# Attention and channel mix on one core: q transposes that write words in sequence, a permuted token order and a new order of the work

## The chip, the cores and the metric

The kernel runs on one core of a Trainium2 chip. The core has five engines that run side by side, each with its own queue of instructions: TensorE (PE, matmuls; PEld is its weight load), VectorE (DVE), ScalarE (ACT), GpSimd (POOL) and SyncE (SP). Data move between DRAM and the on-chip memories by DMA; SP, ACT and POOL issue the DMAs, and 16 DMA engines carry them. The metric is the device time in microseconds, lower is better.

## The reference

For each of 8 batches, 8 heads, 576 tokens and a head size of 64, linear attention without a softmax and a norm over each head's 64 values:

```python
kv = np.einsum('bhsd,bhse->bhde', k, v)
out = np.einsum('bhsd,bhde->bhse', q, kv)
rms = np.sqrt(np.mean(out * out, axis=-1, keepdims=True) + 1e-06)
x = out / rms * g_norm                      # then heads side by side: (8, 576, 512)
```

Then a channel mix, in which each token is blended with the token before it (zero for the first):

```python
x_prev = np.concatenate([np.zeros((B, 1, D)), x[:, :-1, :]], axis=1)
xk = mu_k * x + (1.0 - mu_k) * x_prev
xr = mu_r * x + (1.0 - mu_r) * x_prev
k = np.maximum(xk @ w_k, 0.0)               # 512 -> 1024
v = k * k @ w_v                             # 1024 -> 512
r = 1.0 / (1.0 + np.exp(-(xr @ w_r)))
return r * v
```

Inputs and outputs are float32; inside, the matmuls take bfloat16.

## The kernel before

**Attention, batch by batch.** The names of the pieces carry the batch, then the head group z (z = 0 is heads 0 to 3, z = 1 heads 4 to 7; batch 0 does the two apart, the later batches do both in one piece, "01"), then a half.

- `ld.` loads k, v, q and the weights with a cast to bfloat16 by POOL's DMA queue (L226, L221, L252). For batch 0, z = 0, k and v come as float32 by SP (`ldh`, L236) and are cast by DVE and ACT (`cst`, L128, L130). `small` loads the two mu vectors (each as 4 rows) and the g vector twice (one row each) by SP (L193 to L197); `tr9` turns them on PE (L211) and `cols` copies them (L200).
- `kv` multiplies k and v on PE (L265); `kc` copies the result out of PSUM, `ks` splits it by even and odd d on PE (L271) and `kd` copies it again (the copies at L128 or L130).
- `tq` transposes q on DVE in blocks of 32 x 32 words of 32 bits, a word being two bfloat16 values (L350). A q tile holds 128 partitions: 8 heads of 16 partitions (QP), each with 36 consecutive tokens (QJ) of 64 values. After the transpose a block's 32 columns are 2 heads x 16 partitions for one of the 36 token numbers j. There are two pieces a batch and z group, each with 18 of the 36 j.
- `u` multiplies the transposed q by kv on PE (L281), for one half of the columns at a time. `uc` scales it by g into uT (L134, L136), `sq` squares it (L371), `ss` sums the squares on PE (L396, L380), `rs` takes the reciprocal root on ACT (L286); from batch 2 on, one `rs` serves all heads and `sp` spreads it by 4 DMAs per z on SP (L418).
- `mul` makes x (L393), `d` is x minus the x before it (L298), `mk` and `mr` scale it by mu (L134, L136), `xk` and `xr` add x (L311). They go into rings of 4 batches of columns.

**Channel mix, group by group.** A group is 512 columns of the rings, whatever batch they belong to (9 groups). `k` (L494; group 0 in quarters at L470), `relu` (L453), `ksq` (L481, L504), `r` (L516), `sig` (L526), `v` (L536), `out` = v times sig (L549, L563), `st` stores 128 rows (L444). PSUM has four tiles of two banks in a ring ("ps"); a piece that needs a tile waits until the tile four back has been read.

**The order.** `ORDER` (L15) is a string with the name of each piece in the order in which it is emitted, some with the engine to be used after an @ (A is ACT, D is DVE). Each engine runs its own instructions in this order and waits where data or a buffer are not there. `z:512` is a matmul on zeros that adds nothing and keeps PE busy (L438); there are 38, and `zz` is another (the trace has 39 weight loads and 37 matmul records of them).

In the kernel before, the transpose writes each block's words with a step of 36 words, so that a head's 576 columns stand in the order of the tokens:

```python
dst = get(qT).rearrange("q t r -> q (t r)").bitcast(FP32).rearrange("q (p j) -> q j p", j=QJ)
```

A half of u then needs both transposes of its z, the token before is the column before, and a store writes 128 rows of DRAM that follow each other.

Of the kernel before, what the change touches and what calls it, by code (L numbers as in the profile page):

```python
# [15 lines left out]
ldh.v ldh.k table seta setp perm ld.q0.0 ld.q0.1 ident ld.k0.1 ld.v0.1 ld.wk1 ld.wk0 ld.k1.0 ld.q1.01 ld.v1.0 ld.v1.1 ld.k1.1 ld.wv0 ld.wv1 ld.wr ld.q2.01 ld.v2.01 ld.k2.01 zz cst.v0@D cst.k1@A small setb cst.v1@D tq0.0.1 tq0.0.0 cst.k0@A z:512 z:512 z:512 z:512 z:512 z:512 z:512 z:512 z:512 z:512 z:512 z:512 z:512 z:512 z:512 z:512 z:512 kv0.0 tr9 cols kc0.0@A ks0.0 kd0.0@A z:512 z:512 z:512 z:512 z:512 u0.0.0 sq0.00 u0.0.1 tq0.1.1 uc0.01@A uc0.00@D z:512 z:512 ss0.00 rs0.00 tq0.1.0 z:512 z:512 kv0.1 ld.k3.01 ld.v3.01 ld.q3.01 kc0.1@A sq0.01 z:512 z:512 ks0.1 kd0.1@A z:512 z:512 u0.1.1 u0.1.0 sq0.10 uc0.10@A z:512 z:512 z:512 ss0.10 rs0.10 mul0.00 d0.00 mk0.00@D xk0.00 mr0.00@D z:512 ss0.01 rs0.01 z:512 z:512 z:512 z:512 k0.000 mul0.10 d0.10 sq0.11 ss0.11 mk0.10@D uc0.11@A mul0.01 xk0.10 k0.001 rs0.11 d0.01 mul0.11 d0.11 mk0.01@A mk0.11@A xk0.11 k0.010 xk0.01 tq1.01.1 relu0.00 k0.011 xr0.00 k0.110 k0.111 mr0.11@A xr0.11 relu0.01 ksq0.01 ksq0.00 relu0.11 tq1.01.0 ld.q4.01 k0.100 k0.101 mr0.10@A kv1.01 ld.v4.01 ld.k4.01 relu0.10 ksq0.11 ksq0.10 kc1.01@A ks1.01 kd1.01@A u1.01.1 uc1.11@A uc1.01@D sq1.11 mr0.01@D v0.3.0 xr0.01 u1.01.0 uc1.10@D v0.2.0 sq1.00 uc1.00@D v0.3.1 sq1.01 xr0.10 ss1.0 sq1.10 ss1.3 ss1.1 rs1.0 rs1.1 mul1.0 v0.2.1 d1.0 rs1.3 ss1.2 rs1.2 r0.0 r0.1 sig0.0 r0.2 mul1.1 d1.1 mk1.1@D mr1.1@D xk1.1 tq2.01.1 r0.3 v0.0.0 v0.0.1 mk1.0@A v0.1.0 xk1.0 v0.1.1 mr1.0@A sig0.1 out0.0 k1.4 kv2.01 ld.k5.01 kc2.01@A ks2.01 kd2.01@A tq2.01.0 ld.q5.01 ld.v5.01 u2.01.1 sq2.11 out0.1 uc2.01@D sq2.01 uc2.11@D k1.5 k1.0 u2.01.0 relu1.2 sq2.00 uc2.10@D sq2.10 uc2.00@D k1.1 k1.6 kv3.01 ld.k7.01 ss2 rs2 sp2.0 k1.7 kc3.01@D ks3.01 relu1.0 ksq1.2 sp2.1 xr1.1 xr1.0 kd3.01@A k1.2 k1.3 tq3.01.1 relu1.3 r1.2 relu1.1 tq3.01.0 ksq1.3 ksq1.1 r1.3 sig1.1 u3.01.1 sq3.11 r1.0 st0.0 r1.1 ksq1.0 sig1.0 uc3.01@A v1.3.0 uc3.11@D tq4.01.1 v1.2.0 v1.2.1 sq3.01 u3.01.0 sq3.10 uc3.00@A sq3.00 v1.0.0 v1.1.0 v1.3.1 kv4.01 ld.k6.01 ld.q7.01 ld.v6.01 mul2.0 uc3.10@A ss3 d2.0 mk2.0@D rs3 v1.1.1 v1.0.1 kc4.01@A xk2.0 ks4.01 kd4.01@A mul2.1 d2.1 mk2.1@D xk2.1 k2.4 k2.0 out1.1 mr2.1@D tq4.01.0 ld.q6.01 ld.v7.01 mr2.0@A xr2.0 st0.2 st0.1 out1.0 k2.2 k2.3 relu2.1 xr2.1 k2.1 ksq2.1 sp3.1 st1.3 relu2.0 ksq2.0 k2.5 relu2.2 tq5.01.1 k2.6 k2.7 relu2.3 u4.01.0 uc4.00@D sp3.0 v2.2.0 uc4.10@A r2.2 sq4.00 r2.3 ksq2.2 sig2.1 sq4.10 ksq2.3 r2.0 r2.1 sig2.0 st0.3 v2.3.0 mul3.1 d3.1 tq5.01.0 mul3.0 kv5.01 kc5.01@A d3.0 u4.01.1 sq4.01 uc4.01@D v2.2.1 v2.3.1 sq4.11 st1.0 mk3.0@D mr3.1@A uc4.11@A out2.1 xk3.0 v2.0.0 st1.2 ks5.01 mk3.1@D xk3.1 kd5.01@A v2.1.0 u5.01.0 sq5.00 uc5.10@A mr3.0@D ss4 sq5.10 uc5.00@A v2.1.1 xr3.0 rs4 v2.0.1 k3.0 k3.2 k3.3 relu3.1 tq7.01.1 sp4.0 k3.1 sp4.1 xr3.1 out2.0 st2.1 ksq3.1 relu3.0 r3.2 ksq3.0 r3.3 u5.01.1 r3.0 sig3.1 tq6.01.0 r3.1 uc5.11@D sq5.11 uc5.01@D k3.4 k3.5 st1.1 st2.0 tq6.01.1 mul4.0 d4.0 sig3.0 relu3.2 ksq3.2 sq5.01 k3.6 k3.7 kv6.01 relu3.3 ksq3.3 kc6.01@A kv7.01 kc7.01@D ss5 mr4.0@A rs5 v3.2.0 mk4.0@D st2.2 v3.2.1 ks7.01 kd7.01@A mul4.1 ks6.01 v3.3.0 kd6.01@A v3.3.1 v3.0.0 d4.1 mk4.1@D mr4.1@D xk4.1 u6.01.1 sq6.11 v3.0.1 uc6.01@A sp5.0 v3.1.0 v3.1.1 sq6.01 uc6.11@A u6.01.0 sq6.00 sp5.1 uc6.10@A out3.1 st3.3 xr4.0 xk4.0 k4.2 out3.0 k4.3 sq6.10 relu4.1 st2.3 tq7.01.0 uc6.00@D k4.4 ksq4.1 k4.5 relu4.2 ksq4.2 k4.6 u7.01.1 ss6 xr4.1 rs6 mul5.0 d5.0 uc7.01@D k4.7 relu4.3 mr5.0@D k4.0 k4.1 relu4.0 sp6.0 r4.0 ksq4.3 mul5.1 sq7.11 st3.2 sq7.01 r4.1 sig4.0 r4.2 r4.3 ksq4.0 v4.3.0 d5.1 mr5.1@D v4.3.1 mk5.1@D uc7.11@A mul6.0 v4.2.0 sig4.1 u7.01.0 sq7.10 mk5.0@D xk5.0 v4.2.1 sp6.1 out4.1 st4.2 st4.3 xk5.1 v4.1.0 v4.1.1 mul6.1 sq7.00 ss7 rs7 sp7.1 v4.0.0 d6.1 v4.0.1 uc7.00@A uc7.10@D mk6.1@D d6.0 k5.2 xr5.0 mk6.0@D xk6.0 xk6.1 k5.0 k5.1 xr5.1 mul7.1 sp7.0 k5.4 k5.5 relu5.0 relu5.2 k5.3 relu5.1 ksq5.0 k6.6 ksq5.1 k6.7 relu6.3 mr6.1@D k6.4 v5.2.0 k6.5 relu6.2 k6.0 k6.1 k5.6 d7.1 out4.0 ksq6.3 k5.7 mr7.1@A v5.0.0 mr6.0@D xr6.0 v5.3.0 ksq5.2 relu5.3 relu6.0 ksq6.0 mk7.1@A r5.0 r5.1 xk7.1 sig5.0 r5.2 r5.3 sig5.1 xr6.1 st3.0 ksq5.3 v5.1.0 v5.3.1 v5.0.1 mul7.0 d7.0 mk7.0@A xk7.0 r6.0 r6.1 sig6.0 k6.2 k6.3 relu6.1 ksq6.1 v5.1.1 out5.0 k8.2 r6.2 xr7.1 ksq6.2 k8.3 k7.2 v5.2.1 relu8.1 k7.0 k7.1 r6.3 relu7.0 st3.1 out5.1 ksq7.0 st4.0 st5.1 k7.3 mr7.0@A xr7.0 v6.2.0 v6.3.0 v6.3.1 sig6.1 v6.0.0 v6.2.1 v6.0.1 st4.1 out6.1 st6.3 k7.6 k7.7 relu7.1 ksq7.1 r8.0 relu7.3 ksq7.3 r8.1 sig8.0 k7.4 k8.6 k8.7 relu8.3 k7.5 relu7.2 k8.0 v6.1.0 st6.2 ksq7.2 v6.1.1 v7.1.0 out6.0 ksq8.3 v7.1.1 st6.1 st6.0 v7.0.0 r7.0 r7.1 v7.0.1 sig7.0 v7.2.0 v7.2.1 out7.0 st5.3 ksq8.1 st7.1 k8.4 k8.5 st5.0 r7.2 relu8.2 st7.0 k8.1 relu8.0 r7.3 ksq8.0 sig7.1 r8.2 r8.3 sig8.1 ksq8.2 v8.1.00 v7.3.0 v7.3.1 st5.2 v8.1.10 out8.10 st8.10 out7.1 st7.2 v8.0.00 v8.0.10 out8.00 v8.2.00 v8.2.10 out8.20 v8.3.00 st7.3 v8.3.10 st8.00 v8.3.01 v8.3.11 st8.20 out8.30 st8.30 out8.31 st8.31  # L16
# [40 lines left out]
def kernel(  # L57
# [32 lines left out]
    X0 = 2  # L90
# [12 lines left out]
        "qT": (2, (128, 2 * S, 2), BF16),  # L103
# [66 lines left out]
    def setup_b(_):  # L170
        nc.vector.memset(eps, 1e-6)
        nc.vector.memset(ones, 0.0)
        for e in range(2):
            nc.vector.memset(ones[64 * e:64 * e + 64, 64 * e:64 * e + 64], 1.0 / HD)
        nc.vector.memset(heads, 0.0)
        for e in range(2):
            nc.vector.memset(heads[64 * e:64 * e + 64, e::2], 1.0 / HD)
        for x in xTs:
            nc.vector.memset(x[:, :, 0:X0], 0.0)

# [93 lines left out]
    def u_tiles(pss, kv, qT, zs, c0, c1):  # L274
        for r in range(2):
            for z in zs:
                for y in range(2):
                    for e in range(2):
                        m = 2 * z + y
                        rows_ = slice(32 * m, 32 * m + 32)  # L280
                        nc.tensor.matmul(pss[z][64 * e:64 * e + 64, y, 0:c1 - c0], kv[rows_, r, HD * e:HD * e + HD],  # L281
                                         qT[rows_, S * e + c0:S * e + c1, r], start=(r == 0), stop=(r == 1))
# [5 lines left out]
    x_ready, x_free = {}, {}  # L288
# [3 lines left out]
    def blends(b, z, name, x0, w, deps, mds, dd):  # L292
        xT = xTs[(NZ * b + z) % NX]
        cur, prev = slice(X0 + x0, X0 + x0 + w), slice(X0 - 1 + x0, X0 - 1 + x0 + w)
        cs, r0 = slice(x0, x0 + w), S * (b % RB) + x0
# [23 lines left out]
    PARTS = ((0, GA), (GA, S))  # L319

    def parts(b):
        return PARTS if b == 0 else ((0, HS), (HS, S))

    def attention(b):
# [7 lines left out]
        for zs in zss:  # L332
# [12 lines left out]
            for i in range(2):  # L345
                def tq(_, i=i, part=part):
                    src = qin.t.bitcast(FP32).rearrange("q (j i) -> q j i", i=32)
                    dst = get(qT).rearrange("q t r -> q (t r)").bitcast(FP32).rearrange("q (p j) -> q j p", j=QJ)
# [8 lines left out]
        for i, (c0, c1) in enumerate(parts(b)):  # L357
            for zs in zss:
                p = add(f"u{b}." + "".join(map(str, zs)) + f".{i}", "T", lambda _, zs=zs, i=i, c0=c0, c1=c1: u_tiles(
                    {z: get(us[z][i]) for z in zs}, kv.t, qT.t, zs, c0, c1),  # L360
                    deps=sum(([*qd[z], kvcs[z]] for z in zs), []), bufs=[us[z][i] for z in zs] + [qT, kv])
                for z in zs:
                    pu[(z, i)] = p
        secs = {}
        for z in range(NZ):
            for i, (c0, c1) in enumerate(parts(b)):
# [21 lines left out]
        for z in range(NZ):  # L388
# [51 lines left out]
    out_rows = out.rearrange("b s c -> (b s) c")  # L440
# [164 lines left out]
```

## Time and profile before

| what | value |
|---|---|
| three runs | 202.07, 202.88 and 202.91 us, median 202.88 |
| the profiled execution | 202.8 us as timed; span from first to last instruction 201.0 us |
| granted TensorE clock | 1.000 |
| DVE busy, of it transposes (18 instructions) | 138.3 us, 21.3 us |
| fillers on zeros | 37 matmul records, 12.4 us |
| first matmul of the mix, last matmul ends | 18.57 us, 197.16 us |
| DMA | 30.63 MB in 21016 packets; HBM read 33.56 MB, written 9.44 MB |
| stores | 37 DMAs: 35 of 256 KB and 2 of 128 KB |

How to read the profile's lines: times are microseconds from the start of the span unless "ns" is said. A group's line has the kernel's line, the engine, the operation, the tile written, an arrow and the tiles read, the shapes and the number of instructions; then the busy time and the mean of one in ns; then the idle time of the engine just before them and what ended it. In the slices each digit is the busy share of a fortieth of the span in tenths. A line of the chain has start, duration and what ran. A line of the windows has the window, its length, the busy time of PE, PEld, DVE, ACT and POOL with the number of instructions, the granted clock, the share of the 16 DMA engines' time that was busy, and GB/s. The share can come out a little over 1, since packets on an engine overlap.

### The profile page before, as it was taken

Reading aid. Unit: us, or ns where it says so; the run is one execution under the profiler, and the core shown is the slowest. Engines: PE = TensorE matmul, PEld = TensorE weight load, DVE = VectorE, ACT = ScalarE, POOL = GpSimd, SP = SyncE. Lnnn points to the kernel's source line nnn. Section 1 sums busy time; section 2 is a strip of 40 time slices with the busy share of each in tenths; the row PEclk is TensorE's granted clock in tenths of the full one; section 3 lists DMA queues with packets and bytes.
Section 4 is the critical chain, followed back from the end, with each engine's and each line's share of the span. In section 5 each row is a group of like instructions: output and inputs, shape, how many; then the busy total and the mean of one; then the engine's idle time right before and its main releaser. Section 6 shows DMA issues by size and latency. Waiting matters only on the chain.

```text
span 201.0 us, 4245 instructions
## 1 busy us (share of the span) xinstructions
PE 189.8 (94%) x1743; PEld 93.9 (47%) x1765; DVE 138.3 (69%) x229; ACT 129.5 (64%) x172; POOL 23.1 (12%) x41
## 2 busy tenths in 40 slices
PE   7999779988999999999999999999999999999992
PEld 2545664443544444544545754444444444444451
DVE  1596687997879999797897798998454423133252
ACT  2367978957998579898968689375963554312500
POOL 7743331212100500000000000000000000000000
PEclk9999999999999999999999999999999999999999
DMA  6999999999999999999614242551000202045044
GB/s 212 198 210 216 201 206 216 203 207 219 207 230 257 246 250 265 238 213 194 230 26 94 105 124 50 165 163 57 0 0 0 104 3 104 0 157 209 0 151 166
DMA packets 21016, 30.63 MB, mean 152 GB/s; under 512 B 1917, under 2 KB 14469, under 8 KB 20997
## 3 DMA queue, kind: packets, MB, share of 16 engines
q0 software_dynamic: 11264, 16.19, 45.1%
q1 hardware_dynamic: 9588, 14.03, 21.9%
q8 instruction: 14, 0.23, 0.4%
q10 hardware_dynamic: 144, 0.13, 0.2%
q14 instruction: 6, 0.04, 0.1%
HBM read 33.56 MB, written 9.44 MB: 214 GB/s over the span
## 4 chain that ended last, share of the span: by engine, by line
PE 73%; DMA 9%; DVE 8%; ACT 4%; issue 2%; POOL 2%; SPq 1%; POOLq 0%; DVEq 0%
PE ps L536 27%; PE ps L494 26%; PE ps L516 12%; DMA w_k<-in_moe_w_k_dram 6%; DMA rs<-rsc 3%; PE ps L281 2%; DVE out L549 2%; DVE qT L350 2%; PE ps L470 1%; PE ps L265 1%; ACT relu L453 1%; ACT md L134 1%; DVE xk L311 1%; SPq L418 1%; PE ps L380 1%
## 5 line engine op out<-in xcount | busy, mean ns | idle before, releaser
L536 PE MATMUL ps<-w_v,sqk 128*128 128x512 bf16 (+1 forms) x286 | 65.8, 373 | 0.8 <-issue 0.3
L494 PE MATMUL ps<-xk,w_k 128*128 128x512 bf16 (+1 forms) x282 | 58.2, 355 | 0.7 <-issue 0.3
L453 ACT ACTIVATE relu<-ps 128x1024 bf16<-128x1024 f32 x36 | 36.2, 1022 | 27.9 <-PE ps L494 27.5
L536 PEld LDWEIGHTS <-sqk 128*128 128x128 bf16 x296 | 28.0, 98 | 32.8 <-issue 2.4
L494 PEld LDWEIGHTS <-w_k 128*128 128x128 bf16 x288 | 27.7, 98 | 27.5 <-issue 1.5
L504 DVE TENSOR_TENSOR sqk<-relu 128x1024 bf16<-128x1024 bf16 x32 | 21.6, 687 | 21.5 <-ACT relu L453 21.4
L516 PE MATMUL ps<-w_r,xr 128*128 128x512 bf16 x140 | 33.2, 379 | 0.2
L549 DVE TENSOR_TENSOR out<-ps,sig 128x1024 f32<-128x1024 f32 x16 | 19.5, 1220 | 11.5 <-PE ps L536 7.3
L371 ACT ACTIVATE sq<-ps 128x576 bf16<-128x576 f32 (+2 forms) x32 | 20.3, 650 | 9.1 <-PE ps L281 8.0
L526 ACT ACTIVATE sig<-ps 128x1024 bf16<-128x1024 f32 x18 | 18.3, 1022 | 8.5 <-PE ps L516 7.8
L350 DVE STREAM_TRANSPOSE qT<-q 128x576 f32<-128x576 f32 (+1 forms) x18 | 21.3, 1201 | 2.5 <-DMA q<-in_q_dram 2.1
L516 PEld LDWEIGHTS <-xr 128*128 128x128 bf16 x144 | 13.9, 98 | 16.6 <-issue 0.5
L134 ACT ACTIVATE md<-d,cols 128x576 bf16<-128x576 bf16 (+2 forms) x26 | 16.7, 698 | 0.5 <-DVE d L298 0.5
L144 ACT ACT_TABLE_LOAD x12 | 15.4, 1283 | 0.9 <-PEq L589 0.7
L136 DVE TENSOR_SCALAR uT<-ps,cols 128x576 bf16<-128x576 f32 (+1 forms) x16 | 12.5, 801 | 4.4 <-PE ps L281 2.2
L393 DVE TENSOR_TENSOR xT<-uT,rs 128x1152 bf16<-128x1152 bf16 (+2 forms) x18 | 12.3, 685 | 3.6 <-ACT rs L286 3.5
L311 DVE TENSOR_TENSOR xk<-md,xT 128x1152 bf16<-128x1152 bf16 (+2 forms) x18 | 12.2, 687 | 3.4 <-ACT md L134 3.2
L136 DVE TENSOR_SCALAR md<-d,cols 128x576 bf16<-128x576 bf16 (+2 forms) x46 | 13.9, 354 | 0.2
L438 PE MATMUL ps<-zero 128*128 128x512 bf16 x37 | 12.4, 477 | 1.5 <-DVE zero L164 1.2
L298 DVE TENSOR_TENSOR d<-xT 128x1152 bf16<-128x1152 bf16 (+2 forms) x18 | 12.5, 692 | 0.5
L311 DVE TENSOR_TENSOR xr<-md,xT 128x1152 bf16<-128x1152 bf16 (+2 forms) x18 | 12.1, 683 | 0.7 <-ACT md L134 0.6
L134 ACT ACTIVATE uT<-ps,cols 128x576 bf16<-128x576 f32 (+2 forms) x16 | 11.9, 743 | 0.6 <-PE ps L281 0.6
(47 smaller groups left out, 105.9 us busy)
## 6 DMA issues: line engine op xcount, KB each, us to landing
out_dram<-out SPq DMA_DIRECT2D x35, 256.0 KB, 2.4
q<-in_q_dram POOLq DMA_DIRECT2D x7, 576.0 KB, 21.4
v<-in_v_dram POOLq DMA_DIRECT2D x6, 576.0 KB, 21.9
k<-in_k_dram POOLq DMA_DIRECT2D x6, 576.0 KB, 20.5
rs<-rsc SPq DMA_DIRECT2D x48, 72.0 KB, 2.8
w_k<-in_moe_w_k_dram POOLq DMA_DIRECT2D x2, 512.0 KB, 11.3
w_v<-in_moe_w_v_dram POOLq DMA_DIRECT2D x2, 512.0 KB, 16.1
k<-in_k_dram POOLq DMA_DIRECT2D x3, 288.0 KB, 12.8
```

What stands on the lines that cost most here:

```text
L134: nc.scalar.mul(out=dst, in_=src, mul=col)
L136: nc.vector.tensor_scalar(out=dst, in0=src, scalar1=col, scalar2=None, op0=ALU.mult)
L311: nc.vector.tensor_tensor(out=dst[:, 2 * z:2 * z + 2, r0:r0 + w], in0=md.t[:, :, cs], in1=xT[:, :, cur], op=ALU.add)
L350: nc.vector.transpose(out=dst[part, js, :], in_=src[part, js, :])
L371: sq_ = add("sq" + name, "A", lambda _, ps=ps, sq=sq, cs=cs, w=w: nc.scalar.activation(out=get(sq)[:, :, cs], in_=ps.t[:, :, 0:w], func=AF ...
L453: nc.scalar.activation(out=get(rt), in_=ps.t, func=AF.Relu)
L494: nc.tensor.matmul(get(ps)[:, fc % 2, a0:a1], w_k_sb[:, cc, 128 * fc:128 * fc + 128], xk[:, cc, x0:x0 + a1 - a0], start=(cc == 0), stop=(c ...
L504: nc.vector.tensor_mul(out=get(sqk)[:, 2 * f2:2 * f2 + 2, :], in0=rt.t, in1=rt.t)
L516: nc.tensor.matmul(get(ps)[:, ci % 2, :], xr[:, cc, n0:n0 + 128], w_r_sb[:, cc, :], start=(cc == 0), stop=(cc == NHP - 1))
L526: nc.scalar.activation(out=get(sg), in_=ps.t, func=AF.Sigmoid)
L536: nc.tensor.matmul(get(ps)[:, bank, cs], sqk.t[:, fc, 128 * ci:128 * ci + 128], w_v_sb[:, fc, cs], start=(fc == 0), stop=(fc == NFC - 1))
L549: dv = add(f"out{g}.{c2}", "D", lambda _, ps=ps, sg=sg, ot=ot: nc.vector.tensor_mul(out=get(ot), in0=ps.t, in1=sg.t), deps=ms + [sg_done], ...
```

## The change

The transposes write their words in sequence: a block's 32 columns now stand side by side, and the columns of a head are ordered by j first and partition second. Column c of a batch holds token 36 * (c mod 16) + c // 16. What follows from it:

- The columns of one transpose piece are exactly one half of u, and u waits for this piece alone; u reads 18 runs of 16 columns of its head. Batch 0 is cut into halves of 288 too, where it was cut at 256.
- The token before stands 16 columns back. For the first 16 columns (j = 0) it is in the last 16, one partition lower; `mul` copies these into 15 columns ahead of the tile, by a second small `tensor_mul` for each batch and z.
- In batch 0, whose halves are blended apart, the first 16 columns wait for the second half: they become a third blend (`d0.02`, `mk0.02`, `mr0.02`, `xk0.02`, `xr0.02` and the same for z = 1), and stand last in the ring, so that they belong to group 1.
- A store's 128 rows are now up to 8 values of j with 16 tokens each, 36 rows of DRAM apart. A tile of rows that spans two batches, or the end of batch 0's order, is stored by two or three DMAs: one tile by three and three tiles by two, 42 DMAs in all with the halved last one.
- `ORDER` is another one: the loads come in another order, there are 37 fillers beside `zz` where there were 38, and pieces stand elsewhere all through it, some on the other engine.

The diff, with the ORDER cut to the opening, the first steps of the mix and the end, and broken into lines here:

```diff
 ORDER = """
-ldh.v ldh.k table seta setp perm ld.q0.0 ld.q0.1 ident ld.k0.1 ld.v0.1 ld.wk1 ld.wk0 ld.k1.0 ld.q1.01 ld.v1.0 ld.v1.1 ld.k1.1
-ld.wv0 ld.wv1 ld.wr ld.q2.01 ld.v2.01 ld.k2.01 zz cst.v0@D cst.k1@A small setb cst.v1@D tq0.0.1 tq0.0.0 cst.k0@A (17 z:512)
-kv0.0 tr9 cols kc0.0@A ks0.0 kd0.0@A (5 z:512) u0.0.0 sq0.00 u0.0.1 tq0.1.1 uc0.01@A uc0.00@D
...
-k0.000 mul0.10 d0.10 sq0.11 ss0.11 mk0.10@D uc0.11@A mul0.01 xk0.10 k0.001 rs0.11 d0.01 mul0.11 d0.11 mk0.01@A mk0.11@A xk0.11
-k0.010 xk0.01 tq1.01.1 relu0.00 k0.011 xr0.00 k0.110 k0.111 mr0.11@A xr0.11 relu0.01 ksq0.01 ksq0.00 relu0.11 tq1.01.0 ld.q4.01
-k0.100 k0.101 mr0.10@A kv1.01 ld.v4.01 ld.k4.01 relu0.10 ksq0.11 ksq0.10 kc1.01@A ks1.01 kd1.01@A u1.01.1 uc1.11@A uc1.01@D
-sq1.11 mr0.01@D v0.3.0 xr0.01 u1.01.0
...
-kv2.01 ld.k5.01 kc2.01@A ks2.01 kd2.01@A tq2.01.0 ld.q5.01 ld.v5.01 u2.01.1
...
-v8.1.00 v7.3.0 v7.3.1 st5.2 v8.1.10 out8.10 st8.10 out7.1 st7.2 v8.0.00 v8.0.10 out8.00 v8.2.00 v8.2.10 out8.20 v8.3.00 st7.3
-v8.3.10 st8.00 v8.3.01 v8.3.11 st8.20 out8.30 st8.30 out8.31 st8.31
+ldh.k ldh.v ld.q0.0 table seta setp ident perm ld.q0.1 ld.k0.1 ld.v0.1 ld.wk0 ld.v1.1 ld.wk1 ld.k1.0 ld.v1.0 ld.k1.1 ld.wr
+ld.q1.01 ld.wv0 ld.wv1 ld.k2.01 ld.v2.01 ld.q2.01 small zz (8 z:512) tr9 cst.v0@D cst.k0@A cst.v1@D cst.k1@A (6 z:512)
+kv0.0 setb tq0.0.1 kc0.0@A tq0.1.1 (2 z:512) ks0.0 kd0.0@A (2 z:512) u0.0.1 sq0.01 tq0.0.0 (4 z:512) u0.0.0 cols uc0.01@D sq0.00
...
+ss0.11 k0.000 rs0.11 k0.010 mul0.11 mk0.10@A k0.110 d0.11 xk0.10 mr0.11@A k0.100 mk0.11@D k0.001 xr0.01 xk0.11 xr0.10 k0.011
+relu0.00 xr0.11 k0.101 xr0.00 kv1.01 relu0.10 ksq0.10 kc1.01@A relu0.01 k0.111 ks1.01 mr0.02@D kd1.01@D ksq0.00 r0.2 relu0.11
+r0.3 sig0.1 mk0.02@D r0.0 r0.1 ksq0.11 sig0.0 tq1.01.1 u1.01.1 sq1.11 tq1.01.0 ld.q4.01 ld.v4.01 ld.k4.01 uc1.01@D u1.01.0
...
+kv2.01 ld.k5.01 ld.v5.01 kc2.01@A ks2.01 kd2.01@A tq2.01.0 tq2.01.1 ld.q5.01 mr1.1@A k1.4 k1.5 u2.01.0
...
+kv6.01 relu3.1 relu3.3 mul4.0 d4.0 ksq3.1 ss5
...
+v8.2.00 v8.0.00 v7.0.0 v7.0.1 out7.0 st7.1 st7.0 v8.1.00 v8.2.10 out8.20 st8.20 v8.1.10 v8.0.10 out8.10 st8.10 out8.00 st8.00
+v8.3.00 v8.3.10 out8.30 st8.30 v8.3.01 v8.3.11 out8.31 st8.31
 """
...
-    X0 = 2
+    X0 = QP
...
-        "qT": (2, (128, 2 * S, 2), BF16),
+        "qT": (2, (128, QJ, 2 * QP, 2), BF16),
...
-            nc.vector.memset(x[:, :, 0:X0], 0.0)
+            nc.vector.memset(x[:, :, 0:1], 0.0)
...
-    def u_tiles(pss, kv, qT, zs, c0, c1):
+    def u_tiles(pss, kv, qT, zs, js):
...
-                        nc.tensor.matmul(pss[z][64 * e:64 * e + 64, y, 0:c1 - c0], kv[rows_, r, HD * e:HD * e + HD],
-                                         qT[rows_, S * e + c0:S * e + c1, r], start=(r == 0), stop=(r == 1))
+                        nc.tensor.matmul(pss[z][64 * e:64 * e + 64, y, 0:HS], kv[rows_, r, HD * e:HD * e + HD],
+                                         qT[rows_, js, QP * e:QP * e + QP, r], start=(r == 0), stop=(r == 1))
...
-        cur, prev = slice(X0 + x0, X0 + x0 + w), slice(X0 - 1 + x0, X0 - 1 + x0 + w)
-        cs, r0 = slice(x0, x0 + w), S * (b % RB) + x0
+        cur, prev = slice(X0 + x0, X0 + x0 + w), slice(x0, x0 + w)
+        cs, r0 = slice(x0, x0 + w), S * (b % RB) + ((x0 - QP) % S if b == 0 else x0)
...
-                    dst = get(qT).rearrange("q t r -> q (t r)").bitcast(FP32).rearrange("q (p j) -> q j p", j=QJ)
+                    dst = get(qT).rearrange("q j p r -> q (j p r)").bitcast(FP32).rearrange("q (j p) -> q j p", j=QJ)
...
-                    deps=sum(([*qd[z], kvcs[z]] for z in zs), []), bufs=[us[z][i] for z in zs] + [qT, kv])
+                    deps=sum(([qd[z][i], kvcs[z]] for z in zs), []), bufs=[us[z][i] for z in zs] + [qT, kv])
...
                 nc.vector.tensor_mul(out=xT[:, :, X0 + cs.start:X0 + cs.stop], in0=uT.t[:, :, cs], in1=rs.t[:, :, cs])
+                if cs.stop == S:
+                    nc.vector.tensor_mul(out=xT[:, :, 1:QP], in0=uT.t[:, :, S - QP:S - 1], in1=rs.t[:, :, S - QP:S - 1])
...
+                done = blends(b, z, f"{b}.{z}2", 0, QP, muls, mds[z], dd)
...
-    out_rows = out.rearrange("b s c -> (b s) c")
+    out_jt = out.rearrange("b (t j) c -> b j t c", j=QJ)
...
     def store(g, ci, ot, cs=slice(None), eng=None):
-        row = G * g + 128 * ci
-        (eng or nc.sync).dma_start(out=out_rows[row:row + 128, cs], in_=ot)
+        p = 0
+        while p < 128:
+            b, c = divmod(G * g + 128 * ci + p, S)
+            j = (c // QP + 1) % QJ if b == 0 else c // QP
+            n = min(8 - p // QP, QJ - j, (S - c) // QP)
+            (eng or nc.sync).dma_start(out=out_jt[b, j:j + n, :, cs], in_=ot[p:p + QP * n])
+            p += QP * n
...
```

Words such as "(17 z:512)" stand for so many fillers in a row.

## Prediction

> **What bounds the kernel now.** I read the page's busy table and slices first, then the chain that ended last in order of time, the groups by form, the DMA queues, and windows of the tail. Durations come from the profiled execution: span 201.0 us, 202.8 us as timed, 0.08 below the median of the three runs (202.88), so span + 1.8 is the time.
>
> ```profile
> PE 189.8 (94%) x1743; PEld 93.9 (47%) x1765; DVE 138.3 (69%) x229; ACT 129.5 (64%) x172; POOL 23.1 (12%) x41
> ...
> PE   7999779988999999999999999999999999999992
> ...
> DMA  6999999999999999999614242551000202045044
> ```
>
> PE is full from slice 9 on (45 us); what can be won lies before that, what can be lost in the last slice and wherever a load comes late. The DMA engines are full until 93 us.
>
> ```profile
> 5.93 12.60 DMA w_k<-in_moe_w_k_dram
> 18.53 0.05 issue
> 18.57 1.05 PE ps L470 x8
> ...
> 42.68 1.22 DVE out L549
> ...
> 67.54 7.07 PE ps L494 x32
> ...
> 188.33 8.83 PE ps L536 x48
> 197.16 0.02 issue
> 197.19 0.42 DVE out L563
> ```
>
> The first useful matmul of the mix (piece k0.000) waits for w_k until 18.57; the chain then changes engines until 67.54, and is PE alone from there to 197.16. PE's work from k0.000 on, at 0.216 us for 512 columns (24 matmuls of L536 take 5.18 us of the chain): L536 62.2, L494 55.3, L516 31.1, L470 6.9, the kv, split, u and ss pieces 15.4, together 170.9 us. Without a wait it would end at 189.5; it ends at 197.16. Of the 7.7 us, 1.3 fall after 67.54, where PE never waits: that is what my per-matmul figures are short. **6.4 us are waits before 67.54**: 1.7 within k0 (xk of half 1 late at 23.81), 2.0 between kv1 and the first v piece (copies on ACT with nothing for PE between), 2.0 around kv2 and u2 (copies; PSUM held until DVE has freed it), 0.7 later.
>
> **The change, part by part.**
>
> ```profile
> L350 DVE STREAM_TRANSPOSE qT<-q 128x576 f32<-128x576 f32 x14 | 16.7, 1203 | 0.4 <-PE ps L281 0.4
> ...
> L350 DVE STREAM_TRANSPOSE qT<-q 64x576 f32<-64x576 f32 x4 | 4.6, 1193 | 2.2 <-DMA q<-in_q_dram 2.1
> ...
> L130 DVE CAST v<-xk 128x576 bf16<-128x576 f32 x2 | 0.9, 456 | 3.2 <-DMA xk<-in_v_dram 3.2
> ```
>
> *Transposes.* 1.2 us for 576 words a lane is 2.1 ns a word, written 144 bytes apart. No row shows a sequential write; the bounds are the plain copy of 576 words (0.46) and today's 1.20. I take 0.65, nearer to the copy, since a transpose differs from it only in the order of its words. That is 18 x 0.55 = 10 us of DVE time. The 16 added copies of 15 columns cost at least the 0.06 us of the smallest memset, batch 0's third blend some 14 such instructions more: 2 us. After 67.54 the 8 us are worth nothing: PE is late there, not DVE.
>
> *u halves need one transpose each.* u0.0.0 began at 10.85, 0.14 after the second transpose; its kv copy was done at 10.14. The permuted moving operand (runs of 16 columns) I cost at nothing: doubling the element step costs 11 ns (288 columns: 297 ns at L281 with step 2, 286 at L396 with step 1); by that, at most 0.4 us in all, and no gain.
>
> *New order, opening.* q0.0 goes out first on POOL's queue, ahead of the mask building (it went at 2.33), and so runs beside the two fp32 loads, which landed at 4.6 and 6.0 with the DMA engines 0.85 to 1.2 busy from 2 us on; they and the small loads behind them come up to 1.3 us later, about the 1.4 us that q0.0's bytes take. tr9 now stands ahead of kv0.0 on PE behind nine fillers of 0.43 us (1.19 + 3.9 = 5.0), six fillers follow, and everything on PE is queued behind tr9. If the small loads are there by then, kv0.0 starts after the casts, at 7.8; if they come at 7.2, at 7.6 + 6 x 0.43 = 10.1 (8.14 before). Adding the rows' durations along kv0.0, copy, split, copy, u, square, ss, rs, mul, d, md, xk for both halves and z (ACT is the longest strand), ss0.11 ends and k0.000 starts at 18.7 or 20.8. w_k0, now fifth in the load queue, lands near 16 and no longer matters. From there eight k0 pieces follow without the old wait, k0.111 stands between kv1 and its split, and all of r0 (3.5 us) between the split and u1. Each covers a copy of the list above. w_r, now 11th of the loads, lands near 27, in time for r0; w_v1 is 14th, with the same bytes ahead of it as w_r had, which landed at 34.7. v0.2.1, its first user, has 14.3 us of PE work before it from k0.000; with a square and a sigmoid late on ACT I get 35.1 or 36.2. Behind it stand 156.3 us.
>
> *Sum for PE.* Before: 35.57 (r0.0) plus 157.6 left is 193.1, and 4.0 were lost later (2.7 waits, 1.3 short figures). After: 35.1 or 36.2 plus 156.3 is 191.4 or 192.5; plus 1.3, plus 1.5 for waits left at kv2 and u2 (kv2 and its split still adjoin; k1.4 and k1.5 cover the rest): 194.2 or 195.3. I take 194.8, **2.4 us earlier** than 197.16; one filler less is in it.
>
> *Stores.* They wrote 128 rows of 2 KB in one run; now the DRAM side is 8 runs of j by 16 tokens (4, 3 or 1 by 16 where a tile is split), 41 DMAs on SP for 36.
>
> ```profile
> q1 hardware_dynamic: 9588, 14.03, 21.9%
> ...
> q10 hardware_dynamic: 144, 0.13, 0.2%
> ...
> out_dram<-out SPq DMA_DIRECT2D x35, 256.0 KB, 2.4
> ...
> rs<-rsc SPq DMA_DIRECT2D x48, 72.0 KB, 2.8
> ```
>
> q10 carried one store: 128 rows and 16 packets more, one completion from each engine. q1's data are 36 x 128 + 48 x 64 + 512 (fp32 loads) + 10 (small loads) = 8202 packets; 1386 are left, and 86 x 16 + 10 = 1386: the two mu loads, of 4 rows, ended with 4 completions each, the two g loads, of one row, with 1. **A DMA runs on no more engines than its outer dimension has entries**, so a store with 8 outside should run on 8. The Trainium skill says so too ("DMA: Bandwidth & Descriptors", section "Why a DMA increments its semaphore by 16 and not by 1": the largest number up to 16 that divides the slowest dimension of both sides); the count of 1386 agrees, but no run here shows it for a store.
>
> ```profile
> 155.00:160.00 5.00, 4.95 (x24) 2.25 (x23) 2.71 (x4) 1.84 (x2) 0.00 (x0) 1.00 0.28 105
> 197.00:198.00 1.00, 0.15 (x2) 0.00 (x0) 0.42 (x1) 0.00 (x0) 0.00 (x0) 1.00 0.95 343
> 198.00:199.00 1.00, 0.00 (x0) 0.00 (x0) 0.00 (x0) 0.00 (x0) 0.00 (x0) 1.00 0.55 181
> 199.00:200.00 1.00, 0.00 (x0) 0.00 (x0) 0.00 (x0) 0.00 (x0) 0.00 (x0) 1.00 0.00 0
> ```
>
> Two stores alone: 0.28 x 5 x 16 us over 256 rows is 0.087 us a row, so 0.7 us for a store on 16 engines, 1.4 on 8; rows of 1 KB (0.55 x 16 us, 181 KB) take 0.05: 0.4 and 0.8. At the tail, counted back from PE's end E by 0.864 us a v piece, out7.0 ends at E - 3.9, and a store's packets start some 0.9 us after its product (197.6 to 198.5). From E - 3.0 five full and two half stores share the engines: 5 x 1.4 + 2 x 0.77 = 8.55, to **E + 5.5**; before, E + 1.85 (traffic ends at 199.0). Then 2.0 us to the span's end, as now.
>
> *Loads behind the stores.* From 34.7 to 93.4 the engines moved 18 loads, 16 spread DMAs (rs) and 7 stores. Up to k6, 16th after w_v1 now, I count 16 loads, 22 spreads and 8 stores: 90.0; 0.7 us more a store on eight engines makes 95.6. kv6 is due on PE at 92.3 to 93.5, with all of PE queued behind it: a wait of 0 to 3.3; I take 1.2.
>
> **Forecast:** E = 194.8 + 1.2 = 196.0; span 196.0 + 5.5 + 2.0 = 203.5; time 205.3 us (203.2 to 207.8 by the wait, the opening and a spare 0.5).
>
> **Rivals.**
> *Stores stay on 16 engines* (0.24), if the 8 x 16 rows are counted as 128 for the split. Against it stand the 10 completions; for it, that 4 rows on both sides do not tell which side decides. Then E = 194.8, traffic to E + 1.85: span 198.65, **200.4 us**, faster (198.9 to 202.0). The point from which it decides: the tail's packets take 4.3 us on 16 engines, and PE's 2.4 us are kept only if they end by E + 4.25, 7.25 us after E - 3.0, so on 10 engines or more.
> *Eight engines, but no wait at kv6 and the opening at its best* (0.14): E = 194.2, span 201.7, **203.5**, little changed.
> *The transposes stay at 1.2 us or PE stays at half rate through the opening* (0.06): three transposes and some 20 fillers in line cost up to 2 us at k0.000: E 198, span 205.5, 207.3. On PE's rate: fillers stand 0.43 us apart until 7.14 and some 0.2 after. The Trainium skill ("TensorE: Matmul & The Clock Gate", "Part 1: The HAM clock gate") asks for a busy window of some 3.4 us first, so tr9's wait would prolong the slow part; the sum has both ends from rows.
>
> **Chances.** Forecast 0.56. About 0.5% (1.0 us) is what a measurement here tells from no change. Slower: 0.50 of the forecast, 0.06 of the last rival, 0.02 of the third: 0.58. Faster: 0.21 of the first, 0.03 of the second: 0.24. The same: 0.18. The range of 8 in 10 takes in both signs: 199.6 to 207.8.
>
> **What would show it.** L350 near 650 ns; k0 pieces without a gap; PE's end near 196. Stores: a lower count of completions on q1 (8 for a store), a DMA share near 0.5 while stores run alone, traffic 5 us beyond PE's end. If share and landing stay as now, the store step is wrong; if PE waits at kv6 for DMA, the load step is right. A PE end above 197 refutes the opening.

## The result and the profile after

The changed kernel took **222.16 us** (median of 4 runs, 221.37 to 222.53) against 202.72 for the kernel before on the same chip: a ratio of 1.096 (95% interval 1.092 to 1.100), so it is slower by 19.4 us. The forecast was 205.3 (199.6 to 207.8); it had the sign and missed the size by 16.9. The profiled execution took 221.37 us, its span is 219.6.

First the page of the changed kernel, the slices and the queues:

```profile
PE   7499997999999889449999899999999999999920
...
DMA  6999999999999999653303451314330332111352
...
q1 hardware_dynamic: 9315, 14.03, 22.1%
...
q10 hardware_dynamic: 136, 0.13, 0.2%
```

PE, which was full from slice 9 on, now has holes in slices 14, 15, 17 and 18 (71 to 99 us), and the traffic runs on through slices 39 and 40, where PE has almost nothing. q1 has 9315 packets. By the prediction's count 8202 are data, and the 48 spreads and the small loads end with 48 x 16 + 32 + 10 = 810; 303 are left for 41 stores: 32 whole ones of 8, 23 for the tile in three parts (3 + 16 + 4), 24 for three tiles in two (4 + 4): 303. The store on q10 has 128 rows and 8. So each store ends with as many completions as it has entries outside (the one part of a tile that is a single j has its 16 rows outside).

The chain that ended last in the changed kernel (start, duration, what ran):

```profile
2.81 5.65 DMA rows<-in_g_norm_dram
...
22.69 6.13 PE ps L478 x56
...
61.59 13.87 DMA out_dram<-out
75.55 1.23 DVE out L557
...
79.53 19.78 DMA out_dram<-out
```

The opening hangs on a small load to 8.46 us (5.65), and the mix starts at 22.5 where it started at 18.57. Then 33.7 us of the chain are two stores on their way to DRAM. What they hold up is in the waits of the whole span (total, times, longest):

```profile
DVE out L557 <- DMA out_dram<-out: 24.5, 5, 6.7
...
PE ps L281 <- DVE out L557: 6.8, 2, 6.1
```

and, in the kernel before:

```profile
DVE out L549 <- DMA out_dram<-out: 0.7, 1, 0.7
```

DVE's next product `out` has no free buffer among the three of the tile `out`, because the store that reads the oldest has not landed. DVE stands still; PE's u then has no free PSUM, which DVE should have emptied. Five of these waits were 24.5 us on DVE; before there was one of 0.7. In windows of the changed kernel (after the five engines' busy times: granted clock, DMA share, GB/s):

```profile
90.00:95.00 5.00, 0.10 (x1) 0.10 (x1) 0.06 (x1) 1.03 (x2) 0.00 (x0) 0.92 0.58 135
95.00:100.00 5.00, 3.57 (x23) 1.38 (x24) 2.41 (x3) 1.19 (x2) 0.00 (x0) 0.50 0.44 122
...
210.00:215.00 5.00, 0.14 (x2) 0.00 (x0) 0.42 (x1) 0.00 (x0) 0.00 (x0) 0.87 0.52 176
215.00:220.00 5.00, 0.00 (x0) 0.00 (x0) 0.00 (x0) 0.00 (x0) 0.00 (x0) 0.50 0.24 81
```

From 90 to 95 hardly anything works but the DMA engines, at a share of 0.58. PE stands still from 90.1 to 96.2, and over the window from 95 to 100 its granted clock is 0.50. PE ends at 210.2, and with several stores outstanding the DMA share is 0.52, as of eight engines in sixteen, however many stores wait. For DMAs that SP or ACT issues, the Trainium skill has it that a smaller number of engines is the lowest-numbered ones of the 16 ("DMA: Bandwidth & Descriptors", section "Why a DMA increments its semaphore by 16 and not by 1"); a share that stays at half with a queue of stores agrees with one fixed set of eight, and no run here shows which they are.

Which engines were held up can be read from the share as well. In the changed kernel it falls from 0.94 (88 to 89 us) to 0.59 in the next microsecond and is 0.58 over 89 to 94 and 0.51 over 94 to 99, while the loads' queue q0 still moves 0.28 and 0.31 MB in these two windows. With the 0.52 of the stores at the end beside it, I read this as eight engines that still had stores and loads when the other eight had no work left; the share is a mean and does not name engines. Seven of the 36 tiles had been issued by 80.1 us and an eighth at 89.0. At 256 KB and the 176 GB/s above, 1.49 us each, they are by my estimate 11.9 us of work that only these eight engines had, and the half share lasts some ten.

The transposes, by form:

```profile
L347 DVE STREAM_TRANSPOSE qT<-q 128x576 f32<-128x576 f32 x14 | 10.4, 762 | 0.0
...
L392 DVE TENSOR_TENSOR xT<-uT,rs 128x30 bf16<-128x30 bf16 x16 | 2.7, 169 | 0.0
```

They went from 1203 ns to 762, and the added copies cost 169 ns each; DVE's busy time fell from 138.3 to 134.9 us.

### The profile page after: what moved, and what is told of

Its sections match the earlier page's. It is cut to its first block, busy times and chain, and to the rows that moved or that the text cites. A ratio compares the mean times of both kernels' runs of the same rounds, so it can differ in the third digit from the quotient of the medians.

```text
span 219.6 us, 4282 instructions
## 1 busy us (share of the span) xinstructions
PE 192.9 (88%) x1741; PEld 93.8 (43%) x1764; DVE 134.9 (61%) x261; ACT 130.1 (59%) x170; POOL 23.1 (11%) x41
## 3 DMA queue, kind: packets, MB, share of 16 engines
q1 hardware_dynamic: 9315, 14.03, 22.1%
## 4 chain that ended last, share of the span: by engine, by line
PE 53%; DMA 22%; DVE 8%; ACT 6%; SPq 5%; issue 2%; DVEq 0%
DMA out_dram<-out 19%; PE ps L544 17%; PE ps L502 17%; PE ps L524 8%; PE ps L441 4%; DVE out L557 3%; PE ps L478 3%; SPq L421 3%; DMA rows<-in_g_norm_dram 3%; PE ps L265 2%; ACT relu L461 2%; PE ps L281 2%; SPq L451 1%; DVE qT L347 1%; ACT L144 1%
## 5 line engine op out<-in xcount | busy, mean ns | idle before, releaser
L502 PE MATMUL ps<-xk,w_k 128*128 128x512 bf16 (+1 forms) x280 | 60.5, 362 | 2.2 <-DVE out L557 1.3
L557 DVE TENSOR_TENSOR out<-ps,sig 128x1024 f32<-128x1024 f32 x16 | 19.5, 1219 | 34.8 <-DMA out_dram<-out 24.5
L368 ACT ACTIVATE sq<-ps 128x576 bf16<-128x576 f32 x32 | 20.1, 653 | 10.4 <-PE ps L281 9.5
L534 ACT ACTIVATE sig<-ps 128x1024 bf16<-128x1024 f32 x18 | 18.1, 1022 | 11.9 <-PE ps L524 11.7
L134 ACT ACTIVATE md<-d,cols 128x576 bf16<-128x576 bf16 (+2 forms) x26 | 17.7, 733 | 1.5 <-DVE d L298 1.4
L136 DVE TENSOR_SCALAR uT<-ps,cols 128x576 bf16<-128x576 f32 x15 | 12.1, 813 | 6.6 <-ACT sq L368 4.1
L136 DVE TENSOR_SCALAR md<-d,cols 128x576 bf16<-128x576 bf16 (+3 forms) x54 | 15.1, 326 | 0.4
L281 PE MATMUL ps<-qT,kv 32*64 32x288 bf16 x256 | 8.7, 310 | 7.4 <-DVE out L557 6.8
L134 ACT ACTIVATE uT<-ps,cols 128x576 bf16<-128x576 f32 x17 | 12.4, 740 | 2.1 <-PE ps L281 2.1
L347 DVE STREAM_TRANSPOSE qT<-q 128x576 f32<-128x576 f32 (+1 forms) x18 | 13.5, 764 | 0.1
L298 DVE TENSOR_TENSOR d<-xT 128x1152 bf16<-128x1152 bf16 (+3 forms) x20 | 12.7, 634 | 0.4
L311 DVE TENSOR_TENSOR xk<-md,xT 128x1152 bf16<-128x1152 bf16 (+3 forms) x20 | 12.6, 633 | 0.6 <-ACT md L134 0.3
L390 DVE TENSOR_TENSOR xT<-uT,rs 128x1152 bf16<-128x1152 bf16 (+1 forms) x18 | 12.3, 685 | 0.5 <-ACT rs L286 0.4
## 6 DMA issues: line engine op xcount, KB each, us to landing
w_k<-in_moe_w_k_dram POOLq DMA_DIRECT2D x2, 512.0 KB, 10.7
```

The costliest lines, as they stand in the source:

```text
L134: nc.scalar.mul(out=dst, in_=src, mul=col)
L136: nc.vector.tensor_scalar(out=dst, in0=src, scalar1=col, scalar2=None, op0=ALU.mult)
L368: sq_ = add("sq" + name, "A", lambda _, ps=ps, sq=sq, cs=cs, w=w: nc.scalar.activation(out=get(sq)[:, :, cs], in_=ps.t[:, :, 0:w], func=AF ...
L502: nc.tensor.matmul(get(ps)[:, fc % 2, a0:a1], w_k_sb[:, cc, 128 * fc:128 * fc + 128], xk[:, cc, x0:x0 + a1 - a0], start=(cc == 0), stop=(c ...
L534: nc.scalar.activation(out=get(sg), in_=ps.t, func=AF.Sigmoid)
L557: dv = add(f"out{g}.{c2}", "D", lambda _, ps=ps, sg=sg, ot=ot: nc.vector.tensor_mul(out=get(ot), in0=ps.t, in1=sg.t), deps=ms + [sg_done], ...
```

## The experiments

My theory: the stores on eight engines carry the loss, by landing late while the loads run and by a longer end. The rivals: it is not the number of engines but the scattered rows of DRAM; or it is the new order and layout, which would be slow with any store. Ratios are to the kernel before, with 95% intervals.

**The stores, alone and apart.** First the store function of before in the changed kernel (the values are those of before, the tokens land in permuted rows):

```diff
-    out_jt = out.rearrange("b (t j) c -> b j t c", j=QJ)
+    out_rows = out.rearrange("b s c -> (b s) c")
...
+        row = G * g + 128 * ci
+        (eng or nc.sync).dma_start(out=out_rows[row:row + 128, cs], in_=ot)
```

> The changed kernel with the stores of before: each writes 128 rows that follow each other in DRAM, 37 DMAs; so the tokens of the output stand in the permuted order (this part of the computation is left out). Theory A (a store whose outer dimension is 8 runs on 8 DMA engines, and this, shared with the loads, is most of the loss): no wait of DVE for a store's landing (24.5 us in the changed kernel), PE ends near 198, time 203 us (201 to 206). Theory B (DRAM rows 72 KB apart are slow to write, on however many engines): the same here. Theory C (the new order of the work is the loss, the stores are not): 215 us or more.

Measured: **204.45 us**, ratio 1.009 (1.006 to 1.012). PE ends at 199.6, span 203.5; no product waits for a store. The time from issue to landing of its stores, and of those of the kernel before (minimum, median, longest):

```profile
DMA to landing us min/median/max: 1.8/2.5/10.7
```

```profile
DMA to landing us min/median/max: 1.8/2.4/11.1
```

DVE waits for a store 0 and 0.7 us in these two kernels, so three `out` buffers cover such landings. The first of the windows above, of the kernel with rows in sequence:

```profile
90.00:95.00 5.00, 5.00 (x38) 2.10 (x37) 3.81 (x7) 4.68 (x8) 0.00 (x0) 1.00 1.09 260
```

PE is full where it stood still, and the DMA share is 1.09 where it was 0.58. The store function is worth 222.16 - 204.45 = 17.7 us.

Next the same rows of DRAM as in the changed kernel, 36 apart, but with the 16 tokens as the outer dimension (each row of the tile then lands in another row of the same set):

```diff
-    out_jt = out.rearrange("b (t j) c -> b j t c", j=QJ)
+    out_jt = out.rearrange("b (t j) c -> b t j c", j=QJ)
...
-            (eng or nc.sync).dma_start(out=out_jt[b, j:j + n, :, cs], in_=ot[p:p + QP * n])
+            (eng or nc.sync).dma_start(out=out_jt[b, :, j:j + n, cs], in_=ot[p:p + QP * n])
```

> The changed kernel, with the same DRAM rows in each store and as many DMAs, but the dimension of 16 outside and j inside; so rows go to the wrong tokens within a store (the right order is left out). Theory A: 16 completions a store again, time as with rows in sequence, 203 us (201 to 206). Theory B: the rows lie as far apart in DRAM, 218 us or more. Theory C: 215 us or more.

Measured: **204.72 us**, ratio 1.011 (1.007 to 1.015). q1 of this kernel has 9668 packets, 656 beyond the 8202 and 810: 41 x 16. The median landing of a store is 3.0 us against 2.5 in the experiment above. So the scattered rows cost 0.3 us, which these runs do not tell from nothing, and the count of engines the rest. The issue on SP is as long here as in the changed kernel (median 0.60 and 0.62 us, against 0.42 with rows in sequence), so the longer issue is not the loss either.

Then the kernel before, unchanged but for the changed kernel's form of store (tokens permuted):

> The kernel before with nothing changed but the store function, taken from the changed kernel (8 outside, 16 rows 72 KB apart); so its tokens are written to the wrong rows (the right order of the output is left out). Theory A and B: traffic ends 4 us or more later behind PE's end, and DVE waits for stores while the loads run: 210 to 220 us. Theory C: within 2 us of before.

Measured: **220.28 us**, ratio 1.087 (1.085 to 1.090): 17.4 us more than before, just above the 210 to 220 expected. The new order and layout need not be there for it. The chain of this kernel has one store that took 17.8 us, at 80 us, and ahead of it, from 70 us on, the spreads of rs with 10.0; DVE waits for stores 11.0 us here, not 24.5, so part of the loss goes by the spreads.

**Where the 17.7 us are.** In the changed kernel with the first three groups stored as before and the others on eight engines (tokens of the first groups permuted, some rows not written):

```diff
+        if g < 3:
+            row = G * g + 128 * ci
+            (eng or nc.sync).dma_start(out=out_rows[row:row + 128, cs], in_=ot)
+            return
```

> The changed kernel, in which the stores of the first three groups go out as before (128 rows in sequence, 16 engines; the tokens of these groups then land in permuted rows) and those of groups 3 to 8 on eight engines as in the changed kernel: it parts the price of the load phase from that of the rest. Theory F (the load phase carries nearly all of the later PE end, and the end of the traffic the rest): no wait of DVE on a landed store before 104 us; PE ends at 200 to 202 (e1: 199.6; the changed kernel's waits at 137 and 151 us may stay, 0 to 2 us), the last store lands some 9.5 us after it, and the time is 211 to 213.5. Rival G (eight engines cost as much when they are alone, by the waits at 137 and 151 us): PE ends at 205 or later and the time is 216 or more. Rival H (the stores in the load phase carry the whole price and the tail is their backlog): 204 to 206.

Measured: **211.08 us**, ratio 1.041 (1.039 to 1.044), as theory F had it (its PE end of 200 to 202 was a little late). Its chain still has two waits for stores:

```profile
126.13 4.01 DMA out_dram<-out
...
140.62 5.07 DMA out_dram<-out
```

PE ends at 199.1 all the same, no later than with 16 engines: in the changed kernel's own windows around its waits of this kind (137 to 141 and 152 to 156 us) PE is busy 4.00 and 3.95 of 4 us. Once the loads are done the late stores cost nothing until the end; there the span ends 9.3 us after PE against 3.9. So of the 17.7 us, 222.16 - 211.08 = 11.1 come from the stores of three groups, ten of whose twelve are issued by 92.2 us, that is while the loads run, and 211.08 - 204.45 = 6.6 from the rest. The longer end is 9.3 - 3.9 = 5.4 of it in the profiled executions, which took 210.25 and 205.41 us and so differ by 4.8, not 6.6; what is left is no more than their distance from the medians.

Two more `out` buffers, and the output is the reference's:

```diff
-        "out": (3, (128, 2, C), FP32),
+        "out": (5, (128, 2, C), FP32),
```

> The changed kernel with five buffers for the product that is stored instead of three, everything else and the output as it is. Theory A and B: the stores are as slow, but DVE seldom waits for one to land: PE's idle 10 us between 75 and 160 us shrink to some 2, the tail behind PE's end stays at 9 us, 212 us (208 to 216). Theory C: 221 us.

Measured: **215.51 us**, ratio 1.060 (1.054 to 1.065), in the range of 208 to 216 and 3.5 above its middle. DVE's wait for stores falls from 24.5 to 4.7 us, PE ends at 205.5, still 5.9 after the kernel with rows in sequence. The chain shows why:

```profile
65.63 9.77 DMA rs<-rsc
75.42 9.49 DMA out_dram<-out
85.51 15.19 DMA rs<-rsc
```

The spreads of rs are on SP's queue too, behind the stores; their median landing was 2.8 us before and 5.0 with rows in sequence. Taking one wait away uncovers another on the same engines.

**The dose.** Four outside, in rows in sequence (tokens permuted):

```diff
-        (eng or nc.sync).dma_start(out=out_rows[row:row + 128, cs], in_=ot)
+        (eng or nc.sync).dma_start(out=out_rows[row:row + 128, cs].rearrange("(y x) c -> x y c", x=4), in_=ot)
```

> The kernel of e1, each store of 128 rows in sequence written as 4 x 32 rows with a step of four rows (so the rows of a store land permuted among themselves, and the tokens as in e1): four outside, and by theory A four engines, that is twice the packets on each of half as many. Theory L (in the load phase a store lands when its longest share on one engine has taken its turns behind load packets, so landing grows with the packets an engine gets: at most 10 us at 16 packets in e1, 14 and 20 us at 32 in the changed kernel): some 25 to 40 us at 64, waits of DVE on landed stores of 50 us and more, and each store alone takes about 2.9 us, so that the time is 245 to 290. Rival M (fewer than 16 engines cost a fixed amount, by the issue of 0.62 in place of 0.42 us or by the form of the transfer): the time stays at 218 to 226. q1's completions would be 4 a store, some 160 less than in the changed kernel; if they were 16 as in e1, the test would say nothing.

Measured: **246.21 us**, ratio 1.216 (1.211 to 1.221), and q1 has 9156 packets, 144 beyond the 9012: 36 x 4. With 16, 8 and 4 engines the time is 204.4, 222.2 and 246.2. From the chain of this kernel:

```profile
60.62 22.41 DMA out_dram<-out
...
87.10 17.75 DMA out_dram<-out
...
160.43 8.20 DMA out_dram<-out
```

After the loads the wait is 8.2 us, twice the 4.0 to 4.9 of eight engines. During the loads it is 22.4 and 17.8, not the 25 to 40 that theory L had, and DVE waits 39.5 us for stores, not 50 and more; the time is at the lower edge of its 245 to 290. Rival M, a fixed price, is out. From 16 to 8 engines the longest went from 11.1 (a landing) to 19.8 (a wait in the chain), from 8 to 4 only to 22.4, where theory L has it double each time. The share shows the same picture as with eight, at half the height: over 88 to 95 us it is 0.30, with 0.19 MB of loads on q0. What sets the length of the landing at four engines stays open.

**Two ways round it, both with the reference's output.** One j a store, 16 outside, eight times the issues:

```diff
-            n = min(8 - p // QP, QJ - j, (S - c) // QP)
+            n = 1
```

> The changed kernel with each store cut into eight, one j each: the outermost dimension of a piece is then its 16 rows, so its packets should lie on 16 engines, at eight times the issues (about 290 on SP's queue in place of 39, 32 KB each). The output is the reference's. Theory A (the count of engines is the price, in the load phase and at the end): the waits of DVE on a landed store at 61 and 79 us go, and PE ends near 200 as in e2; what is left is the issuing, 8 x 0.42 to 0.62 us = 3.4 to 5 us a store, which the four stores of a group of some 20 us can just bear, but not the five of the last 10 us: they end some 5 to 12 us later than e2's, 209 to 216 us. If the pieces were held back behind loads just as the whole stores were, the waits of DVE stay and the time is 222 or more.

Measured: **247.84 us**, ratio 1.220 (1.215 to 1.225); expected 209 to 216. The landing was as theory A had it (median 1.7, at most 6.2 us), but the queue was not. The timeline of SP in this kernel (start, duration, line, tile, number of issues):

```profile
141.56 7.38 SPq L451 DMA_DIRECT2D out_dram<-out  x16
149.50 6.01 SPq L421 DMA_DIRECT2D rs<-rsc  x8
155.61 9.54 SPq L451 DMA_DIRECT2D out_dram<-out  x20
```

In this stretch SP issues without a pause, 0.46 to 0.48 us a piece and 0.75 a spread: 288 pieces and 48 spreads are some 170 us of one queue (288 x 0.47 + 48 x 0.75), and they can begin only at 60 us. I had set four stores against a group's 20 us and forgotten the spreads' 6 us. The wait for buffers came back by another road (32.9 us on DVE).

The stores on POOL's queue once its loads are issued, with tr9 moved as in the next experiment:

> The changed kernel with tr9 behind kv0.0 and, once the last load is issued, its stores issued by POOL's software queue instead of SP's; the last tile's two stay where they were; the output is the reference's. If that queue spreads 8 x 16 rows over all 16 engines, or over eight that change from store to store: no wait of DVE for a store after 70 us, 203 us (201 to 206). If it uses the same eight engines: 212 us or more.

Measured: **223.46 us**, ratio 1.103 (1.101 to 1.106). The time is in the range given for the same eight engines (212 or more), but not for that reason: in the end the DMA share is 0.78 (window 210 to 215), above what eight showed. Stores issued while the loads are outstanding land late, after up to 23.2 us, with one wait of DVE of 13.8; that they stand behind the loads on the same queue is my reading, and no run parts it from other causes. No gain.

**The opening and the transposes, without the price of the stores.** On the kernel with rows in sequence, `tr9` moved from before the casts of k and v (`cst`) to behind `kv0.0` in the order:

> The changed kernel with rows stored in sequence (the tokens of the output stand in permuted order) and tr9 moved from ahead of the first casts to behind kv0.0, as before. Theory D (with the stores put right, what is left of the loss is tr9's wait for the small loads, which holds back kv0.0 to 11 us): kv0.0 starts near 7.8 us, k0.000 near 20, time 201.5 us (200.3 to 202.7). Rival E (the later waits of the new order and w_v1's landing set the pace, the opening's 3 us are lost again): 203.7 us or more.

Measured: **203.13 us**, ratio 1.002 (1.000 to 1.005), between theory D's 200.3 to 202.7 and rival E's 203.7 or more. The mix starts at 18.27 in place of 22.92, 4.65 us sooner; the median is 1.3 us shorter. The profiled execution took 205.05 us, 1.9 above the median, so its PE end of 199.4 says little, and what waits in it may wait longer than usual. Its chain and its waits:

```profile
19.14 17.72 DMA k<-in_k_dram
37.15 25.98 DMA k<-in_k_dram
```

```profile
PEld L265 <- DMA k<-in_k_dram: 3.4, 1, 3.4
```

In this execution PE comes to kv4 before k4 does. To see whether another order of the loads keeps the gain, k4 and v4 went ahead of q4 and q4's first transpose behind kv4:

> The kernel of e5 (store function of before, the g and mu transposes behind kv0.0), with the loads of k4 and v4 issued right after kv1, ahead of q4, and the transposes of q4 moved behind kv4: the bytes are the same and in another order. Theory J (what the transposes and the mended opening gain is given back at kv4, where PE waits 3.4 us for k4's load): k4 lands some 5 us sooner, that wait goes, and 203.1 becomes 200 to 201.5. Rival K (the load phase is bound by its bytes and DVE's transposes: another load is late in its place): 202.5 to 203.7, with a wait for q4 or for a transpose as long as that for k4.

Measured: **202.81 us**, ratio 1.001 (1.000 to 1.003). The wait for k4 is gone, PE ends at 197.0 (197.2 before the change), and the chain goes through q's loads instead:

```profile
12.13 16.38 DMA q<-in_q_dram
29.06 22.05 DMA q<-in_q_dram
```

Theory J's wait went; its time of 200 to 201.5 did not come, K's did. Against the kernel with rows in sequence, an opening 4.65 us quicker is worth 1.3 to 1.6 us, and against the kernel before nothing: the chain then goes through the loads, which move at 201 to 282 GB/s through slice 19 (95 us) and come no sooner.

Each transpose issued twice, on the kernel with tr9 moved:

> As tr9 behind kv with rows in sequence, but each transpose is issued twice (the second writes the same again): 0.77 us more of DVE 18 times, more than the 0.44 us that sequential writing saves each. If the transposes' time counts only in the opening: at most 1.5 us more than with one. If DVE is late through the first 70 us: 3 us more or above.

Measured: **207.62 us**, ratio 1.024 (1.021 to 1.027): 4.5 us for 13.9 us of added transposes, so the branch of 3 us or above. Most of PE's waits for a transpose lie before 60 us (4.3 of 5.2 for the weight loads of u, 2.4 of 2.9 for its matmuls). So DVE is near the path in the first 60 us, and what a transpose costs matters mainly there.

The order of before with the new layout and rows in sequence (the third blends after `xr0.10`):

> The kernel before's ORDER with the changed layout (sequential transposes, u waiting for one transpose, batch 0 in halves of 288 with a third blend put in behind xr0.10), rows stored in sequence, so the output's tokens stand in permuted order. Theory D: the layout alone gains little in an order made for the old one, 202.5 us (201.5 to 204), and the new order's gain shows only against this. Rival E: this is the fastest of the four, below 202.

Measured: **202.92 us**, ratio 1.000 (0.999 to 1.002), as theory D had it. Faster transposes alone, in an order made for slow ones, are worth nothing that shows. No version here beats the kernel before.

## Why the prediction missed

The step that failed is the one headed "Loads behind the stores", with the sum that hangs on it. In spans, from the forecast's 203.5 to the 219.6 measured:

| step | forecast | measured | difference |
|---|---|---|---|
| PE's end without the price of the stores | 194.8 | 199.6 (rows in sequence) | +4.8 |
| what the stores add to it | 1.2, as a wait at kv6 | 10.6, as waits for `out` buffers (210.2 - 199.6) | +9.4 |
| from PE's end to the span's end | 7.5 | 9.4 | +1.9 |

The profiled execution with rows in sequence is 1.0 above its median and that of the changed kernel 0.8 below, so a row of the table can be out by that much.

- **Transposes:** right in kind, 0.76 where I took 0.65, within the bounds; "worth nothing after 67.54" held. That DVE was not late before either was not said, and the doubled transposes show that it nearly is. The small copies cost 0.17 us, above my floor of 0.06, and hid.
- **u's permuted operand:** 301 ns on average in the kernel with rows in sequence against 297: 256 x 4 ns is 1.0 us of PE over the span, more than the 0.4 I gave it, and small.
- **The opening:** refuted, by the prediction's own mark (PE's end above 197), also without the stores. I bounded the rows' arrival by 5.0 and 7.2 us; the small load landed at 8.46. kv0.0 began at 11.55 (7.8 or 10.1 forecast), k0 at 22.5 (18.7 or 20.8) and v0.2.1 at 38.6 (35.1 or 36.2). k0 ran without a gap, as forecast. The steps between held: from the landing to kv0.0 3.1 us (0.4 and six fillers of 0.43 in the forecast), from kv0.0 to k0 11.0 (10.9 or 10.7). With rows in sequence v0.2.1 is at 38.97, so 2.8 to 3.9 of the 4.8 us in the table are there already; where the rest went is not settled. With tr9 moved, k0 comes at 18.3 and the opening is what I had forecast at its best, and the kernel gains only 1.3 us by it: I had put the waits before 67.54 down to copies and PSUM, and did not ask whether the loads would be there if PE came earlier. They are not: the chain of both kernels with tr9 moved runs through loads of k or q until 51 to 63 us.
- **Stores on eight engines:** right, shown for stores by 8, 4 and 16 completions and by shares of 0.52. 256 KB at 176 GB/s are 1.49 us a store, where I took 1.4.
- **The price while loads run:** I spread the stores' longer time over the sum of all bytes (0.7 us a store) and looked for its victim among the loads, at kv6. After the opening no piece on PE waited for a load. The extra time falls on eight engines alone, and by the share they still had loads and stores at 89 to 99 us when the others had none. The victim is the store: the chain waits 13.9 and 19.8 us for it, where a landing on 16 engines took 11.1 at most. Three `out` buffers covered the 11.1 and not the 13.9; DVE waits, PSUM stays full, PE waits, and the spreads on SP's queue come late as well. A longer landing of an asynchronous store is free only while its buffer ring covers it, and I had costed the ring at nothing without naming it.
- **The end:** 1.9 us short. At 1.49 a store the six stores are 0.5 longer; from 205 to 210 us only 107 GB/s moved, so the stores also began later than my count from PE's end had them. Which of them was held, I did not settle.
- **Rivals:** the stores did not stay on 16 engines (the price of that rival, 200.4, would have been 204.4, as the first experiment shows, so its gain was wrong too). "No wait at kv6" came true, and did not help. The slow-opening rival named the right place, for another cause: the transposes became quick, and the small load was late. The half rate that it feared did last (the six fillers behind tr9 took 2.67 us), and the forecast's later branch had counted it.
- **A reading of the kernel before:** its chain is not PE alone from 67.54 on; from 185.94 to 188.33 it is on ACT and DVE. Nothing in the sum hangs on it.

## What to carry to other kernels

Look at the outer dimension of each DMA that a change of layout touches: it may halve the engines that carry it, and a store that shares these engines with loads in flight then lands so late that its buffer ring becomes the bound, and with a longer ring whatever is queued behind it, here the spreads. Cost a slower store at the place where its buffer is wanted again, and name what stands behind that wait on each engine. When some of the DMA engines carry more than the others, look for the stage in which the busy share drops to their part while loads are still moving. A quicker opening is worth only what the loads behind it allow; ask which load is late next before counting it.

## What was not expected of the hardware

- A store under load: a landing of 10.7 to 11.1 us at most on 16 engines, waits in the chain of 13.9 and 19.8 us on eight, 22.4 and 17.8 on four; after the loads, waits of 4.0 to 5.1 on eight and 8.1 to 8.2 on four.
- Issue on SP: a store in rows in sequence takes 0.42 us (median), in scattered rows with eight outside 0.62 and with 16 outside 0.60, a piece of 16 rows 0.42.
- PE stood still from 90.1 to 96.2 us, and its granted clock was 0.50 over 95 to 100, so this wait cost more than its length.
